# The buffers gh and gl are laid behind wsp, at the lower end of SBUF

## The chip, the cores and the metric

One core of a Trainium2 chip runs the kernel. The metric is device microseconds from start to end of one execution; the time shown is the median of three runs.

## What is computed

Three layers in a row, all in float32, from the reference (cut):

```
# q, k, v: (2, 8, 768, 64); block 32, window 16, nb = 24
k_sum = k.reshape(B, H, nb, block, D).max(axis=3)
v_sum = v.reshape(B, H, nb, block, D).mean(axis=3)
scores_l = scale * q @ k^T, kept where |i - j| < 16
scores_s = scale * q @ k_sum^T + log(block)
a = softmax of both side by side;  attn = a @ concat(v, v_sum)
x = attn.transpose(0, 2, 1, 3).reshape(1536, 512)
x = ((x @ w_a) * (x @ w_b)) @ w_out          # 512 -> 1536 -> 512
h = x @ w_in;  out = (h - tanh(h)) @ w_out2  # 512 -> 2048 -> 512
```

So it is a banded attention with block summaries, then a gated MLP, then a second MLP. The weights come to the kernel as words of 64 bits, which it decodes to float32 itself.

## The kernel before

**Precision by splitting.** A large matmul takes fp32r operands. Each operand is kept as two tiles, a rounded high part and the rest as a low part, and a product is three matmuls: high x high, high x low, low x high (lines 366 to 370, 397 to 398, 458 to 459). The tile `wsp` (four buffers of 4 KB per partition) holds the two parts of one weight tile, made by `split_w` (lines 181 to 186: ACT writes the high part, DVE or POOL the low one). XA and XB (16 KB each) hold the two parts of the activations of one block. `gh` and `gl` (two buffers of 2 KB each) hold the high and low parts of the hidden activations between the two products of an MLP; line 363 (ACT) writes `gh` and line 364 (DVE) writes `gl`.

**Positions.** The 1536 rows are three blocks of 512. The list `pos` (lines 478 to 507) is the order of work on TensorE. One position is twelve matmuls of 128x128 by 512 on one weight tile:

- `pos_a` and `pos_b` (lines 373 and 381): x times a tile of w_a or w_b into the PSUM banks pa and pb, through `proj` on line 370. Weights are wsp, the moving operand is XA (blocks 0 and 2) or XB (block 1). `pos_b` then multiplies both and splits the result into gh and gl.
- `pos_o` (line 390): the second product of the first MLP, line 398. Weights are wsp, the moving operand is gh or gl. There are 12 such positions in each block, 36 in all.
- `pos_h` (line 419): the first product of the second MLP, again line 370, into pa, pb, ps and pt in turn. Activations are in XB (blocks 0 and 2) or XA (block 1). The activation function h - tanh(h) is worked out on ACT and DVE, and the result g is split by `late_hi_lo` (line 444) one position later.
- `pos_o2` (line 448): the second product of the second MLP, line 459. Here the activations are the weights of the matmul and wsp is the moving operand. There are 48, one for each group G, two groups behind `pos_h`.

Where g of the second MLP is kept goes by the group's number:

```
439  gs[1000 + G] = pair((("gh", 2), ("gl", 2)) if G % 3 < 2 else (("vw", 3), ("vw", 3)))
```

`vw` is a buffer of the attention stage (three of 2 KB) that is free by then. So of every three groups two use gh and gl, and the third uses two of the vw buffers.

**Stages.** The first 45 us or so are the head: loads, and the first eight attention units, whose order on every engine is written out by hand (SEQ, line 771). In the head, gh and gl also serve as `at` tiles of four units, and ta and tg as `e` tiles (lines 667 and 700). Then positions run; until about 290 us the remaining 16 attention units are put in between, by the table `at` that `plan` fills (lines 520 to 575), and weights are loaded on SP's queue, decoded on ACT, DVE and POOL (lines 146 to 168) and, in part, written back and loaded again later. From position 0 on SP keeps the order as written while the framework's scheduler orders the other engines; from position 72 on all engines keep the order as written (line 498).

**Where buffers lie.** All tiles come from one pool. A tag gets its buffers, side by side, at the moment it is first used in the program, and each tag follows the one before it. By the program's allocation, in KB of the 224 KB of a partition, before the change:

```
qbd   24.3   wsp  28.3 to 44.3    XB  44.3 to 60.3    kw  60.3
w     64.3   vw  136.3 to 142.3   XA 142.3 to 158.3   kt 158.3
x20a 170.7   stage 178.7          x21a 190.7          e  198.7
ta   202.9   tg  206.9 to 210.9   gh 210.9 to 214.9   gl 214.9 to 218.9
at   218.9 to 222.9
```

Within 256 bytes, wsp, XB, vw and XA start at byte 32; gh and gl (and all tags from x20a on, as kt is 12,672 bytes) start at byte 160.

Of the kernel before, what the change touches and what calls it, by code (L numbers as in the profile page):

```python
# [12 lines left out]
F32R = mybir.dt.float32r  # L13
# [26 lines left out]
def band_attention_moe_kernel(ctx: ExitStack, tc: tile.TileContext, q, k, v, w_a, w_b, w_out, w_in, w_out2, out):  # L40
# [11 lines left out]
    TB = 512  # L52
# [10 lines left out]
    def st(shape, tag, bufs=1, dt=F32):  # L63
        return sb.tile(shape, dt, tag=tag, bufs=bufs, name=tag)
# [10 lines left out]
    mavp = st([128, KW + 2 * NB - 8], "qn", 3)  # L75
    qbd = st([128, 2, NP, 128], "qbd")
    qbd2 = st([128, 2, NP, 128], "wsp", 4)

    xb = st([128, 2 * KC * TB], "XB")
    kq = xb[:, 0:3072].rearrange("p (c h d) -> p c h d", c=NC, h=H)  # L80
# [753 lines left out]
```

## Time and profile before

| what | value |
| --- | --- |
| median of three runs | 667.28 us (665.36 to 667.33) |
| span of the profiled execution | 664.0 us |
| PE busy (matmuls) | 643.2 us, 97% |
| PE weight loads busy | 518.1 us, 78% |
| DVE busy | 501.9 us, 76% |
| ACT busy | 476.2 us, 72% |
| POOL busy | 209.7 us, 32% |
| granted TensorE clock, mean | 0.997 |

The profile is of one execution; its span is the time from the first to the last instruction, and the runs' times contain a little more around it. Busy shares are averages over stages. A matmul's duration in the profile reaches from its start to its modelled end and overlaps the next one, so twelve matmuls of some 390 ns each take 2.7 us together; the pace is read from the starts, or from the chain in order of time, where a row "PE acc L459 x12" is one position.

### The profile page before, as it was taken

What the parts mean: (1) busy time and instruction counts of PE and PEld (TensorE: products, weight loads), DVE (VectorE), ACT (ScalarE), POOL (GpSimd) and SP (SyncE); (2) the same over time, 40 slices, a digit from 0 to 9 for tenths busy, and PEclk for the clock granted to TensorE, in tenths of its full rate; (3) what the DMA queues carried; (4) which work ended last, traced back from release to release, by engine and by line L of the source; (5) the groups of instructions that cost most, each with busy time, mean ns of one, the idle gap of its engine ahead of it and who ended that gap; (6) DMA issues with size and microseconds to landing.
All of it is one profiled execution on the core that took longest, in us unless ns stands there. A gap on an engine that the chain in (4) does not pass through costs nothing.

```text
span 664.0 us, 9626 instructions
## 1 busy us (share of the span) xinstructions
PE 643.2 (97%) x3240; PEld 518.1 (78%) x3240; DVE 501.9 (76%) x999; ACT 476.2 (72%) x1000; POOL 209.7 (32%) x221
## 2 busy tenths in 40 slices
PE   7778999999899999999999999999999999999997
PEld 5567876888588888888888888888888888888885
DVE  5899999888675777647877748877777877777775
ACT  4899897798677687636655547777777777777774
POOL 6761231122000010101111135554444544444441
PEclk9989999999999999999999999999999999999999
DMA  9996984563414545513444200000010000000001
GB/s 203 243 237 179 250 226 128 169 216 107 102 66 124 169 152 155 144 47 112 149 140 152 68 1 0 1 0 1 1 63 1 0 1 0 32 33 1 1 0 64
DMA packets 84781, 62.11 MB, mean 94 GB/s; under 512 B 51892, under 2 KB 75444, under 8 KB 84732
## 3 DMA queue, kind: packets, MB, share of 16 engines
q1 hardware_dynamic: 84732, 61.50, 33.4%
q8 instruction: 25, 0.41, 0.3%
q14 instruction: 24, 0.20, 0.1%
HBM read 54.00 MB, written 7.34 MB: 92 GB/s over the span
## 4 chain that ended last, share of the span: by engine, by line
PE 82%; DVE 7%; ACT 4%; DMA 3%; issue 2%; SPq 1%; POOL 0%; DVEq 0%; ACTq 0%
PE acc L459 20%; PE pb L370 18%; PE pa L370 17%; PE acc L398 12%; PE pt L370 5%; PE ps L370 5%; DMA stage<-in_moe_w_in_dram 2%; PE ps L288 1%; DVE w L164 1%; PE ps L340 1%; DVE w L165 1%; PE pt L240 1%; PE pt L327 1%; DMA x20a<-in_q_dram 1%; SPq L610 1%
## 5 line engine op out<-in xcount | busy, mean ns | idle before, releaser
L185 POOL TENSOR_TENSOR wsp<-w,wsp 128x512 fp32r<-128x512 f32 x97 | 127.5, 1333 | 143.7 <-ACT wsp L184 143.7
L184 ACT ACTIVATE wsp<-w 128x512 fp32r<-128x512 f32 x201 | 121.4, 622 | 18.8 <-PE acc L398 8.6
L185 DVE TENSOR_TENSOR wsp<-w,wsp 128x512 fp32r<-128x512 f32 x104 | 75.0, 723 | 42.5 <-ACT wsp L184 42.3
L179 POOL TENSOR_SCALAR w<-w 128x512 f32<-128x512 f32 x52 | 42.0, 811 | 184.3 <-ACT w L154 184.1
L398 PE MATMUL acc<-gh,wsp 128*128 128x512 f32 x288 | 97.8, 398 | 0.5 <-ACT gh L363 0.5
L370 PE MATMUL pa<-XA,wsp 128*128 128x512 f32 x336 | 85.0, 400 | 2.8 <-ACT XA L720 2.1
L370 PE MATMUL pb<-XA,wsp 128*128 128x512 f32 x336 | 84.1, 394 | 1.4 <-DVE tg L386 1.4
L459 PE MATMUL acc<-wsp,gh 128*128 128x512 f32 x256 | 80.5, 396 | 0.0
L370 PEld LDWEIGHTS pa<-XA,wsp 128*128 128x128 f32 x336 | 63.5, 191 | 18.3 <-ACT XA L720 2.4
L370 PEld LDWEIGHTS pb<-XA,wsp 128*128 128x128 f32 x336 | 62.1, 188 | 15.0 <-ACT x21a L155 1.6
L363 ACT ACTIVATE gh<-tg 128x512 fp32r<-128x512 f32 x68 | 42.4, 623 | 33.3 <-DVE tg L386 32.9
L398 PEld LDWEIGHTS acc<-gh,wsp 128*128 128x128 f32 x288 | 53.7, 188 | 12.0 <-ACT gh L363 0.6
L370 PE MATMUL pb<-XB,wsp 128*128 128x512 f32 x240 | 61.0, 396 | 0.0
L370 PE MATMUL pa<-XB,wsp 128*128 128x512 f32 x240 | 60.4, 395 | 0.0
L398 PE MATMUL acc<-gl,wsp 128*128 128x512 f32 x144 | 57.3, 399 | 1.1 <-DVE gl L364 1.1
L459 PEld LDWEIGHTS acc<-wsp,gh 128*128 128x128 f32 x256 | 48.2, 188 | 11.1
L364 DVE TENSOR_TENSOR gl<-tg,gh 128x512 fp32r<-128x512 f32 x68 | 46.6, 686 | 9.4 <-ACT gh L363 9.3
L370 PEld LDWEIGHTS pa<-XB,wsp 128*128 128x128 f32 x240 | 44.5, 188 | 9.8 <-DVE XB L348 0.2
L370 PEld LDWEIGHTS pb<-XB,wsp 128*128 128x128 f32 x240 | 44.4, 188 | 9.5
L459 PE MATMUL acc<-wsp,gl 128*128 128x512 f32 x128 | 50.5, 394 | 0.0
L459 PE MATMUL acc<-wsp,vw 128*128 128x512 f32 x192 | 46.5, 390 | 0.0
L459 PEld LDWEIGHTS acc<-wsp,vw 128*128 128x128 f32 x192 | 35.9, 188 | 8.1 <-DVE vw L364 0.4
(304 smaller groups left out, 1176.0 us busy)
## 6 DMA issues: line engine op xcount, KB each, us to landing
stage<-in_moe_w_out_dram SPq DMA_DIRECT2D x19, 512.0 KB, 3.8
stage<-in_moe_w_in_dram SPq DMA_DIRECT2D x16, 512.0 KB, 5.6
stage<-in_moe_w_a_dram SPq DMA_DIRECT2D x8, 512.0 KB, 4.9
w<-wsc SPq DMA_DIRECT2D x16, 256.0 KB, 3.5
vw<-in_v_dram SPq DMA_DIRECT2D x19, 192.0 KB, 3.2
stage<-in_moe_w_b_dram SPq DMA_DIRECT2D x7, 512.0 KB, 5.7
wsc<-x21a SPq DMA_DIRECT2D x8, 256.0 KB, 4.9
wsc<-x21b SPq DMA_DIRECT2D x8, 256.0 KB, 5.1
```

The costliest lines, as they stand in the source:

```text
L164: nc.vector.scalar_tensor_tensor(r, t[:, :, 1], -0x40000000, r, op0=ALU.bitwise_and, op1=ALU.bitwise_or)
L165: nc.vector.tensor_tensor(r, r, t[:, :, 0], op=ALU.add)
L179: nc.gpsimd.tensor_scalar(rf, rf, HI_HI, HI_LO, op0=ALU.min, op1=ALU.max)
L184: nc.scalar.activation(s[:, 0, :], r, AF.Copy)
L185: eng.tensor_tensor(s[:, 1, :], r, s[:, 0, :].bitcast(F32), op=ALU.subtract)
L240: mm(pp, mavg[:, NB - 4 - 4 * c : 2 * NB - 4 - 4 * c], vch.pop(c).rearrange("p h d -> p (h d)"), start=(c == 0), stop=(c == NC - 1),)
L288: mm(pp[:, p, 0:NK], qt[:, p, :], kw[:, p, :], start=True, stop=True)
L363: nc.scalar.activation(dst[0], src, AF.Copy)
L364: eng.tensor_tensor(dst[1], src, dst[0].bitcast(F32), op=ALU.subtract)
L370: mm(dst, w, xx, start=(kk == 0 and n == 0), stop=(kk == KC - 1 and n == 2))
L398: mm(acc[blk][d][:, c0:c1], w, t, start=(f == 0 and c0 == 0 and n == 0), stop=(f == F1 - 1 and n == 2))
L459: mm(a[c], g[:, cs], s[:, i, :], start=(f == 0 and n == 0), stop=(f == F2 - 1 and n == 2))
```

## The change

Four tiles are reserved right after wsp is first used, two of gh and two of gl, and nothing is ever written to or read from these four. As the tags are then first used there, their buffers lie behind wsp (gh 44.3 to 48.3 KB, gl 48.3 to 52.3 KB), and every tag from XB to tg lies 8 KB higher: XB 52.3 to 68.3, vw 144.3 to 150.3, XA 150.3 to 166.3, ta and tg 210.9 to 218.9 KB. `at` stays where it was. No instruction is added, taken away or altered but for the addresses.

```
@@ -75,6 +75,9 @@
     mavp = st([128, KW + 2 * NB - 8], "qn", 3)
     qbd = st([128, 2, NP, 128], "qbd")
     qbd2 = st([128, 2, NP, 128], "wsp", 4)
+
+    for tag in ("gh", "gh", "gl", "gl"):
+        st([128, TB], tag, 2, F32R)
 
     xb = st([128, 2 * KC * TB], "XB")
     kq = xb[:, 0:3072].rearrange("p (c h d) -> p c h d", c=NC, h=H)
```

## Rows read from the trace of the kernel before

**Rows 1.** The page's first line: the profiled execution
```profile
span 664.0 us, 9626 instructions
```

**Rows 2.** Stretches: us, PE, PEld, DVE, ACT, POOL busy, clock, DMA share, GB/s
```profile
45.00:175.00 130.00, 126.30 (x684) 98.47 (x683) 119.00 (x267) 108.33 (x250) 30.30 (x35) 0.99 0.65 179
175.00:290.00 115.00, 113.48 (x665) 92.41 (x664) 75.39 (x192) 81.13 (x199) 10.38 (x15) 1.00 0.45 132
290.00:400.00 110.00, 110.00 (x481) 90.10 (x480) 78.03 (x121) 60.70 (x107) 18.48 (x22) 1.00 0.28 94
400.00:660.00 260.00, 260.00 (x1130) 211.90 (x1128) 194.87 (x297) 193.58 (x341) 120.52 (x92) 1.00 0.03 10
```

**Rows 3.** Groups by line, PE, 403:651 us (xcount, busy us, mean ns, idle)
```profile
L459 PE MATMUL acc<-wsp,gh 128*128 128x512 f32 x240 | 75.5, 396 | 0.0
L459 PE MATMUL acc<-wsp,gl 128*128 128x512 f32 x120 | 47.3, 394 | 0.0
L459 PE MATMUL acc<-wsp,vw 128*128 128x512 f32 x180 | 43.2, 389 | 0.0
L370 PE MATMUL pt<-XB,wsp 128*128 128x512 f32 x96 | 23.3, 391 | 0.0
```

**Rows 4.** Chain in order of time, 403:436 us (start us, us, what)
```profile
403.13 2.80 PE acc L459 x12
405.92 2.76 PE pt L370 x12
408.68 2.80 PE acc L459 x12
411.48 2.75 PE pa L370 x12
414.23 2.72 PE acc L459 x12
416.95 2.73 PE pb L370 x12
419.67 2.80 PE acc L459 x12
```

**Rows 5.** Timeline of PE, 403:422 us: two kinds of L459 position
```profile
408.52 0.64 PE L459 MATMUL acc<-wsp,gh 128*128 128x512 f32 x2
...
414.06 2.88 PE L459 MATMUL acc<-wsp,vw 128*128 128x512 f32 x12
```

**Rows 6.** Chain in order of time, 293:320 us
```profile
298.63 2.79 PE acc L398 x12
301.43 2.73 PE pa L370 x12
304.16 2.72 PE pb L370 x12
```

**Rows 7.** One position near the end, columns as in rows 2
```profile
654.20:656.70 2.50, 2.50 (x12) 1.88 (x10) 1.76 (x3) 0.74 (x2) 0.00 (x0) 1.00 0.00 0
```

**Rows 8.** Timeline of PE, 654:657 us, the same position
```profile
654.42 0.40 PE L459 MATMUL acc<-wsp,gl 128*128 128x512 f32 x1
...
656.52 0.40 PE L459 MATMUL acc<-wsp,gl 128*128 128x512 f32 x1
```

**Rows 9.** Line 398 alone: us, PE, PEld busy, clock, DMA share, GB/s
```profile
45.00:175.00 130.00, 38.68 (x144) 26.14 (x144) 0.99 0.65 179
175.00:290.00 115.00, 31.40 (x120) 22.11 (x120) 1.00 0.45 132
290.00:400.00 110.00, 41.36 (x168) 31.53 (x168) 1.00 0.28 94
```

**Rows 10.** Groups by line, whole run: line 459 on gh
```profile
L459 PE MATMUL acc<-wsp,gh 128*128 128x512 f32 x256 | 80.5, 396 | 0.0
```

**Rows 11.** Chain, shares by line, 45:175 us and then 175:290 us
```profile
by line: PE pb L370 13.2%; PE acc L398 10.9%; PE pa L370 10.6%; DMA stage<-in_moe_w_in_dram 8.1%; DVE w L164 6.8%; issue 6.3%; DVE w L165 4.6%; PE pt L240 4.0%; DVE wsp L185 3.9%; DMA stage<-in_moe_w_b_dram 3.2%; DVE w L161 2.5%; PE ps L288
...
by line: PE pa L370 29.4%; PE pb L370 29.0%; PE acc L398 24.5%; PE ps L288 6.2%; PE ps L340 4.9%; PE pt L327 3.0%; PE pt L269 1.8%; ACT wsp L184 0.5%; issue 0.5%; ACT at L330 0.4%
```

More of the change, by code (lines that the diff above doesn't have):

```diff
@@ L77, in band_attention_moe_kernel @@
     qbd2 = st([128, 2, NP, 128], "wsp", 4)
+    for tag in ("gh", "gh", "gl", "gl"):
+        st([128, TB], tag, 2, F32R)
     xb = st([128, 2 * KC * TB], "XB")
```

## The prediction

> **What bounds the kernel now.** I read the page's first line, then busy time by stretch, then the groups of one stretch on PE, and last the chain in order of time, where one position of the kernel (twelve matmuls on one weight tile) stands as one row. The profiled execution spans 664.0 us [rows 1]; the median of the three runs is 667.28 us, 3.3 us above that span, and I carry this difference along unchanged. The reader should see in the stretches that PE is busy for all of 290 to 660 us at full granted clock, while DVE, ACT and POOL stay at 75% or less [rows 2]. From 175 to 290 us it is busy for 98.7%, and the chain there is 98.8% PE [rows 2, 11]. Only from 45 to 175 us does the chain also run through weight loads and decoding; the PE entries with a share beside them add to 39% [rows 11]. So for most of the run the time is the number of matmuls times their pace, and a change that moves no instruction can matter only by changing that pace.
>
> The pace is not the same everywhere. In the second MLP a position of line 459 takes 2.80 us twice and 2.72 us the third time [rows 4]. The timeline tells which is which: the position from 408.5 us takes its weights from gh and gl, the one from 414.1 us from vw [rows 5]. Line 439 sends each third group through vw and the other two through gh and gl. The twelve matmuls are the same in count, size, moving operand (wsp) and PSUM banks (acc). By groups, a matmul lasts 396 ns on gh, 394 ns on gl and 389 ns on vw, over 540 of them and with no idle time ahead [rows 3]. The position of line 370 that follows gh takes 2.75 to 2.76 us, the one after vw 2.73 us [rows 4], so part of the cost is paid by the neighbour: its mean is 391 ns [rows 3]. In the first MLP gh and gl are the moving operand instead of the weights, and it is the same: 2.79 us on line 398 against 2.72 us for pb, and 2.73 us for the pa in between [rows 6]. What gh and gl have in common in both places is where they lie: 210.9 to 218.9 KB, near the top of the 224 KB of a partition, while wsp, XB, vw and XA, which run at 2.72 us per position, lie between 28.3 and 158.3 KB. (gh and gl also start 160 bytes behind a multiple of 256, those others 32 bytes behind one; the change alters both properties, so the forecast needs no choice between them.)
>
> That it is contention with the engines that fill these buffers is hard to hold: near the end, in a position on gh with POOL idle and ACT busy for 0.74 of 2.50 us [rows 7], nine matmuls still take 2.10 us [rows 8], which is 0.233 us each or 2.80 us for twelve, as in the busy middle.
>
> **The change, part by part.** It adds four tile reservations with no instruction behind them, so nothing is issued, no DMA joins SP's queue, and no wait is added that anything could queue behind: the two buffers of each tag are reserved twice, which leaves their alternation as it was. I price this at nothing; if it did alter a wait, the stretches in which PE never idles would show it at once.
>
> *gh and gl move from 210.9 to 44.3 KB.* They take the lower half of the place where XB lies today. With wsp weights, XB is the moving operand there and its matmuls cost 391 ns even with gh's tail in the mean [rows 3]; so this very place is known to be good for the moving operand. For the weights the nearest row is vw at 389 ns [rows 3]. I take 2.72 us for every position, the row that both uses share, and no better: no row shows a faster one.
>
> - Second MLP: three groups from 403.13 to 419.67 us take 16.54 us [rows 4]; six positions at 2.72 us are 16.32 us. The 48 groups hold sixteen such triples: 16 x 0.22 = 3.5 us. Gh alone has 256 matmuls on line 459 [rows 10], eight per position, so 32 positions, which agrees.
> - First MLP from 290 us: 2.79 + 2.73 + 2.72 = 8.24 us [rows 6] against 8.16 us, and 0.01 us from rounding as the next triple starts 8.25 us later; 0.09 us for each of 168/12 = 14 positions [rows 9]: 1.3 us.
> - 175 to 290 us: 120/12 = 10 positions [rows 9], 0.09 us each, nearly all on the chain [rows 11]: 0.9 us.
> - 45 to 175 us: 144/12 = 12 positions [rows 9], 1.1 us at most. Where PE saves time here, it often just waits for weights still being loaded and decoded, so I take the 39% that the chain shows of PE [rows 11]: 0.4 us. Bounds are nothing and 1.1 us.
>
> Sum: 3.5 + 1.3 + 0.9 + 0.4 = 6.1 us. The span would be 657.9 us, and the median 667.3 - 6.1 = 661.2 us. The cover is thin elsewhere: with PE 1% faster, ACT and DVE (75% and below after 290 us [rows 2]) are still not next; what is late next is PE again.
>
> *Everything from XB up to tg moves up by 8 KB* (`at`, above gl, stays). XA goes from 142.3 to 150.3 KB, so its upper half, the low parts of x, enters 158.3 to 166.3 KB, where no matmul of this size reads today. vw ends at 150.3 KB, below XA's present end. If gh's cost comes from height, the bound lies somewhere between 158.3 and 210.9 KB, and the 8 KB that XA newly enters are 15% of that; if it comes from the 160 bytes, XA keeps its 32 and nothing happens. I price XA at nothing and keep the other end as a rival. ta and tg now reach into gh's old place, but the large matmuls never read them, and no row shows ACT or DVE caring about the place. In the first 45 us gh and gl also serve four attention units; at 0.08 us each this is 0.3 us at the very most, either way, and I put it at nothing.
>
> A rule speaks against all of this. The Trainium skill, page "SBUF — State Buffer", section "Who interferes with whom", says that PE never waits on anyone because its ports are its own, and the page gives no price for an address. By that the move would be worth nothing and the time 667.3 us. The row with POOL idle agrees that it is no contention, but the pair of gh and vw positions does not agree that place is free. Its chance is that of the first rival.
>
> **The rivals.**
>
> *The place is not the cause.* Something else that goes with gh and gl (which instructions fill them, which semaphores their matmuls see) makes 2.80 us, and it moves with them: 667.3 us. For it: no engine's own row prices an address. Against it: the two MLPs use gh in opposite roles, with different producers' timing, and pay nearly the same 0.07 to 0.08 us in the position itself [rows 4, 6]; vw is filled by the same two lines 363 and 364. Chance 0.09.
>
> *XA's upper half becomes what gh was.* The first MLP has 48 pa and pb positions on XA (blocks 0 and 2, twelve each twice) and the second MLP 16 (block 1): 64. Four of twelve matmuls read the low part, so the price is 64 x 4/12 x 0.08 = 1.7 us if only they pay, and 64 x 0.09 = 5.8 us if each upset costs a whole position: 662.9 to 667.0 us. For it: the following positions do pay for an upset [rows 4]. Against it: only 15% of the possible bounds. Chance 0.08, most of it still faster by over 2 us.
>
> *The two reads of one matmul collide, and it is slower.* gh and gl then lie wall to wall with wsp, and each of the 36 + 32 = 68 positions reads one from each. If PE's weight read and its moving read hinder each other when both come from one part of memory, these positions keep a cost. It decides at 2.83 us: from there 68 x 0.03 = 2 us are lost beyond today's 2.80. If the present excess of 0.08 us doubled, it would be 68 x 0.08 = 5.4 us and 672.7 us. Against it: XB with wsp is just such a pair of neighbours today and costs 391 ns like the others [rows 3]. Chance 0.04.
>
> *The reservation does not do what it says,* and gh and gl stay on top or the order of instructions changes a little: about 667.3 us. Chance 0.02.
>
> **How the numbers follow.** The forecast has 0.77. A measurement of this kernel can tell about 0.3%, 2 us, from no change. Faster by more than that (below 665.3 us): the forecast and 0.06 of XA's case, 0.83. Within: 0.09 + 0.02 and 0.02 of XA's case, 0.13. Slower: the collision, 0.04. The lower end takes the 45 to 175 us stretch in full (660.5 us) and the spread of the runs, whose lowest is 1.9 us under the median: 658.8 us. The upper end takes in about half of XA's case: 665.0 us. Left out are the two cases without effect, the collision and the rest of XA, 0.19 in all.
>
> **What would show it.** Right: every line 459 position at 2.72 us, whether on gh or vw; line 398 at 2.72 us; gh, gl and vw groups within 1 ns of each other; PE's instruction count and the order of work unchanged; the stretch from 290 us shorter by 4.8 us. XA's case would show as 2.75 us or more for pa and pb on XA but 2.72 us on XB. The collision would show as line 398 and 459 above 2.80 us. The forecast is wrong if gh's positions still stand at 2.80 us, or if PE, now faster, shows new idle time ahead of line 370 or 459 behind ACT's wsp (line 184).

## The result and the profile after

The changed kernel takes 660.88 us (median of six runs, 659.02 to 661.90), the kernel before 666.79 us in the six runs made by then: 5.9 us less, ratio 0.9916 (95% interval 0.9898 to 0.9934). The forecast was 661.2 us, faster. The profiled execution spans 657.7 us against 664.0 us [rows 1], 6.3 us less. Every engine runs the same instructions in the same order as before; line numbers are higher by 3.

The page's first line, and its busy times by engine:

```profile
span 657.7 us, 9626 instructions
...
PE 637.2 (97%) x3240; PEld 518.0 (79%) x3240; DVE 502.4 (76%) x999; ACT 475.3 (72%) x1000; POOL 209.3 (32%) x221
```

PE's busy time falls from 643.2 to 637.2 us with the same 3240 matmuls; no other engine's changes by over 1 us. So the matmuls themselves became cheaper. Groups by line on PE, 400 to 648 us, as in [rows 3]:

```profile
L462 PE MATMUL acc<-wsp,gh 128*128 128x512 f32 x250 | 77.0, 389 | 0.0
L462 PE MATMUL acc<-wsp,gl 128*128 128x512 f32 x125 | 48.7, 389 | 0.0
L462 PE MATMUL acc<-wsp,vw 128*128 128x512 f32 x180 | 43.2, 389 | 0.0
L373 PE MATMUL pt<-XB,wsp 128*128 128x512 f32 x96 | 23.1, 389 | 0.0
```

gh (396 ns before), gl (394) and the neighbours on XB (391) are all at the 389 ns that vw alone had. The chain in order of time, around 300 us and from 400 us, as in [rows 6] and [rows 4]:

```profile
296.82 2.72 PE acc L401 x12
299.54 2.72 PE pa L373 x12
302.26 2.72 PE pb L373 x12
...
400.18 2.72 PE acc L462 x12
402.90 2.72 PE pt L373 x12
405.62 2.72 PE acc L462 x12
408.34 2.72 PE pa L373 x12
411.06 2.72 PE acc L462 x12
413.78 2.72 PE pb L373 x12
```

Every position from 290 us up to the last two is at 2.72 us; the two in three at 2.80 us and their followers at 2.75 to 2.76 us are gone.

Where the time was won is read by laying the same piece of work side by side. First the chain before, at the transposes of line 269 that end the wait near 175 us, then the chain after:

```profile
177.27 0.58 PE pt L269 x4
```
```profile
176.24 0.59 PE pt L272 x4
```

That is 1.0 us by then, in this pair of executions. The L398 position that starts at 298.63 us [rows 6] starts at 296.82 us: 1.8 us. The first one of line 459, at 403.13 us [rows 4], starts at 400.18 us: 2.95 us. And the last, on the timeline of PE before and then after:

```profile
656.78 3.29 PE L459 MATMUL acc<-wsp,vw 128*128 128x512 f32 x12
```
```profile
650.44 3.33 PE L462 MATMUL acc<-wsp,vw 128*128 128x512 f32 x12
```

6.3 us, and that stays to the end. By stretch the gain is 1.0, 0.8, 1.1 and 3.4 us.

### The profile page after: what moved, and what is told of

Read it like the earlier page. It is cut to its first block, busy times and chain, and to the rows that moved or that the text cites. A ratio compares the mean times of both kernels' runs of the same rounds, so it can differ in the third digit from the quotient of the medians.

```text
span 657.7 us, 9626 instructions
## 1 busy us (share of the span) xinstructions
PE 637.2 (97%) x3240; PEld 518.0 (79%) x3240; DVE 502.4 (76%) x999; ACT 475.3 (72%) x1000; POOL 209.3 (32%) x221
## 4 chain that ended last, share of the span: by engine, by line
PE 87%; DVE 6%; ACT 3%; DMA 2%; issue 1%; SPq 1%; POOL 0%; DVEq 0%
PE acc L462 20%; PE pb L373 19%; PE pa L373 18%; PE acc L401 14%; PE pt L373 5%; PE ps L373 5%; PE ps L291 2%; PE ps L343 1%; DMA stage<-in_moe_w_in_dram 1%; PE pt L330 1%; PE pt L243 1%; DMA x20a<-in_q_dram 1%; SPq L613 1%; DVE w L167 1%; DVE w L168 1%
## 5 line engine op out<-in xcount | busy, mean ns | idle before, releaser
L462 PE MATMUL acc<-wsp,gh 128*128 128x512 f32 x256 | 78.8, 389 | 0.0
```

Source lines behind the costliest of these rows:

```text
L462: mm(a[c], g[:, cs], s[:, i, :], start=(f == 0 and n == 0), stop=(f == F2 - 1 and n == 2))
```

## The experiments

The forecast left open what about the place counts. The theory **height** says that gh and gl were slow because they lay near the top. The rival **offset** says that it was because they started 160 bytes behind a multiple of 256, where wsp, XB, vw and XA start at 32. The change altered both. In all kernels below no instruction is added, taken away or reordered; only addresses differ, through reservations that nothing uses. All ratios are to the kernel before, run on the same chip.

**Same height, other offset** (the kernel before, with):

```
         elif n.startswith("T3e"):
             i = int(n[3])
+            if i == 2:
+                st([128, 32], "pad")
```

> The kernel before with 128 unused bytes ahead of gh: gh and gl stay near the top (211.0 to 219.0 KB) but start 32 bytes behind a multiple of 256 instead of 160; nothing else moves but at. Theory height: positions of lines 398 and 459 on gh and gl stay at 2.80 us, ratio to before 1.00. Rival offset (the 160 bytes are the cause): they fall to 2.72 us, ratio 0.991, some 661 us.

Measured: 660.61 us, ratio 0.9917 (0.9897 to 0.9938). Its chain, around 300 us and from 400 us:

```profile
298.42 2.72 PE acc L398 x12
301.14 2.72 PE pa L370 x12
...
401.78 2.72 PE acc L459 x12
404.50 2.72 PE pt L370 x12
```

128 unused bytes do all that the change does, with gh and gl still at the top. Height falls.

**Low, but at 160** (the changed kernel, with one line ahead of the new loop and one behind it):

```
+    st([128, 32], "pad0")
     for tag in ("gh", "gh", "gl", "gl"):
         st([128, TB], tag, 2, F32R)
+    st([128, 32], "pad1")
```

> The changed kernel with 128 unused bytes ahead of gh and 128 behind gl: gh and gl lie low (44.4 to 52.4 KB) but start 160 bytes behind a multiple of 256; XB, vw and XA keep their 32. Theory height: all positions 2.72 us as after the change, ratio to before 0.991. Rival offset: positions on gh and gl are 2.80 us again, ratio to before 1.00.

Measured: 665.83 us, ratio 1.0009 (0.9996 to 1.0021). Its chain shows the positions of before, digit for digit, at the low place:

```profile
299.04 2.79 PE acc L403 x12
301.83 2.73 PE pa L375 x12
...
403.53 2.80 PE acc L464 x12
406.33 2.76 PE pt L375 x12
```

**Everything from wsp up moved by 128 bytes** (the kernel before, with one line ahead of wsp; wsp, XB, vw and XA then start at 160, gh and gl at 32):

```
+    st([128, 32], "pad")
     qbd2 = st([128, 2, NP, 128], "wsp", 4)
```

> The kernel before with 128 unused bytes ahead of wsp: everything from wsp up moves by 128 bytes, so wsp, XB, vw and XA start at 160 and gh and gl, still near the top, at 32. Theory height: as before, 2.80 us on gh and gl, 2.72 us elsewhere, ratio 1.00. Rival offset taken by itself: gh no longer costs as such, but every position reads wsp at 160, so all 201 positions go to about 2.80 us, some 10 us slower, ratio 1.015. Rival offset of the two operands against each other: unchanged, ratio 1.00, as the difference stays 128.

Measured: 665.33 us, ratio 0.9999 (0.9985 to 1.0012). In its chain gh, now at 32, still costs 2.80 us, and vw against wsp, both now at 160, costs 2.72 us:

```profile
404.20 2.80 PE acc L460 x12
...
415.30 2.72 PE acc L460 x12
```

So neither operand's own start counts, but the difference between the two.

**How large a difference.** gh and gl get buffers of 2304 bytes in the changed kernel and are used from byte s on; here s = 32 (8 elements):

```
     for tag in ("gh", "gh", "gl", "gl"):
-        st([128, TB], tag, 2, F32R)
+        st([128, TB + 64], tag, 2, F32R)
...
-        return [st([128, TB], t, n, F32R) for t, n in tags]
+        return [st([128, TB + 64], t, n, F32R)[:, 8 : 8 + TB] if t[0] == "g" else st([128, TB], t, n, F32R) for t, n in tags]
```

> The changed kernel, gh and gl in buffers of 2304 bytes and used from byte 32 on, so that they start 32 bytes further behind a multiple of 256 than wsp. Theory bit (only whether both operands start in the same half of 256 bytes counts): both start in the lower half, 2.72 us, ratio to before 0.991. Theory distance (the cost grows with the difference up to 128): part of the cost, positions between 2.72 and 2.80 us. Theory any (every difference costs): 2.80 us, ratio 1.00.

> The same with gh and gl used from byte 64 on, 64 bytes off wsp. Theory bit: 2.72 us, ratio 0.991. Theory distance: about half of the cost, 2.76 us, ratio 0.995. Theory any: 2.80 us, ratio 1.00.

> The same with gh and gl used from byte 192 on, 192 bytes off wsp. Theory bit: the other half of 256 bytes, 2.80 us, ratio 1.00. Theory distance (192 is 64 the other way round): as the 64-byte run, 2.76 us. Theory any: 2.80 us, ratio 1.00.

> The same with gh and gl used from byte 256 on. If the cost goes by 256 bytes, there is none: 2.72 us, ratio 0.991. If it goes by 512 or more, 2.80 us, ratio 1.00. It is also the control of the longer buffers, which move XB and what follows by another 1 KB.

> The changed kernel, gh and gl in buffers of 2304 bytes and used from byte 16 on. Theory any, down to single bytes: 2.80 us as with 32 bytes, ratio to before 1.00. Theory grain (only steps of 32 bytes count): 2.72 us, ratio 0.991.

Measured ratios: s = 16: 0.9937 (0.9918 to 0.9957); 32: 1.0007 (0.9995 to 1.0020); 64: 0.9995 (0.9979 to 1.0011); 192: 0.9967 (0.9953 to 0.9981); 256: 0.9911 (0.9885 to 0.9937). Positions from the chains, line 401 (gh moving) first, line 462 (gh as weights) second; s = 16, 32, 64, 192 and 256 in this order:

```profile
290.28 2.78 PE acc L401 x12
...
403.02 2.72 PE acc L462 x12
```
```profile
291.88 2.80 PE acc L401 x12
...
405.09 2.79 PE acc L462 x12
```
```profile
289.70 2.76 PE acc L401 x12
...
402.53 2.80 PE acc L462 x12
```
```profile
298.28 2.80 PE acc L401 x12
...
402.94 2.75 PE acc L462 x12
```
```profile
296.26 2.72 PE acc L401 x12
...
399.62 2.72 PE acc L462 x12
```

None of the four theories on record holds whole. "Bit" fails at 32 and 64, "distance" at 32 (which costs as much as 128), "any" at 16, 64 and 192, where one of the two lines is cheaper or free, and "grain" at 16, where line 401 pays. What fits is a difference with a sign: call d the moving operand's start minus the weights' start, modulo 256. Line 401 has d = s, line 462 has d = 256 - s. Then the rows order themselves: d = 0: 2.72 us; 16: 2.78; 32: 2.80; 64: 2.76 (as moving, s = 64) and 2.75 (as weights, s = 192); 128: 2.79 and 2.80 (the kernel before); 192: 2.80 in both roles; 224: 2.79; 240: 2.72. At 64, 128 and 192 the two roles agree to 0.01 us, so there it is the difference and not the role that sets the cost. At 16, 32, 224 and 240 only one role was seen, so that 240 is free as such, and not only with gh as weights, is not shown. This ordering was found after the runs and not forecast.

**Another buffer out of step** (the changed kernel, with one line ahead of XA; kt and what follows move along, gh and gl don't):

```
+        st([128, 32], "pad0")
         XAv = st([128, 4, 2 * TB], "XA")
```

> The changed kernel with 128 unused bytes ahead of XA: XA, whose positions are at 2.72 us in both kernels, starts at 160, and gh, gl, vw, XB and wsp at 32. Theory difference of the two operands of a matmul, whichever buffer: the 64 positions on XA go to 2.80 us with what follows them, XB, gh and vw keep 2.72 us unless they come right behind one; 64 x 0.08 = 5.1 us slower than after the change, ratio to before some 0.998. Rival (only gh and gl are sensitive): ratio 0.991.

Measured: 664.56 us, ratio 0.9975 (0.9960 to 0.9990). In the chain the positions on XA now cost what those on gh did, while XB's at 400 us are untouched:

```profile
292.51 2.79 PE pa L373 x12
295.30 2.80 PE pb L373 x12
...
400.59 2.72 PE ps L373 x12
403.31 2.72 PE acc L462 x12
...
476.75 2.79 PE pa L373 x12
479.54 2.73 PE acc L462 x12
```

So the sensitivity is not gh's and gl's own. By the two ratios to the kernel before, 0.9975 and 0.9916, it costs some 3.9 us, less than the 5.1 us expected. That sum counts in full the 24 positions on XA that run before 175 us, where PE also waits for weights; from 176 us on, where the other 40 positions on XA lie, matmul by matmul the run falls 3.4 us behind the changed kernel, and 40 x 0.08 is 3.2 us.

**Every position out of step** (the changed kernel, with wsp alone at 160):

```
+    st([128, 32], "pad0")
     qbd2 = st([128, 2, NP, 128], "wsp", 4)
 
+    st([128, 32], "pad1")
     for tag in ("gh", "gh", "gl", "gl"):
```

> The changed kernel with 128 unused bytes ahead of wsp and 128 behind it: wsp alone starts at 160, gh, gl, XB, vw and XA at 32, so that every one of the 201 positions reads two operands that differ by 128. Theory difference: every position costs 2.79 to 2.80 us, also on vw and XB, 201 x 0.075 = 15 us over the changed kernel, some 676 us, ratio to before 1.014. Rival (wsp's start does not count, only that of the activations): as after the change, ratio 0.991.

Measured: 672.85 us, ratio 1.0109 (1.0089 to 1.0129), some 13 us over the changed kernel by the two ratios. The pace is as expected to 0.01 us, on gh, vw and XB alike; by the timeline the row from 417.85 us is on vw:

```profile
406.68 2.79 PE acc L464 x12
409.47 2.79 PE pt L375 x12
412.26 2.80 PE acc L464 x12
...
417.85 2.80 PE acc L464 x12
420.65 2.80 PE pb L375 x12
```

The sum was put too high (15 us). From 290 us on, matmul by matmul, the run falls 9.7 us behind the changed kernel, and the 133 positions there at 0.075 us make 10.0 us; ahead of 290 us it falls 3.7 us behind, where the other 71 positions, counted in full, would make 5.3 us. Part of PE's time there is a wait for something else [rows 11]. (The matmuls make 204 positions, 2448 / 12, and not 201.)

**Does the common start count?** (the changed kernel, with 224 unused bytes ahead of wsp: `st([128, 56], "pad")`)

> The changed kernel with 224 unused bytes ahead of wsp: wsp, gh, gl, XB, vw and XA all start on a multiple of 256. Theory difference: nothing changes, 2.72 us, ratio to before 0.991. Rival (the distance from a multiple of 256 counts too): the common pace itself moves off 2.72 us; 1 ns for each of 2448 matmuls would be 2.4 us.

Measured: 660.12 us, ratio 0.9902 (0.9870 to 0.9933). In its chain a position on gh is at 2.72 us (the line above wsp makes line 462 into 463):

```profile
401.58 2.72 PE acc L463 x12
```

The common start does not count.

**The other large buffers that PE reads, aligned too** (the changed kernel, with 160 unused bytes ahead of ident, 96 behind it and 128 behind kt):

> The changed kernel with unused bytes ahead of and behind ident and behind kt, so that every large buffer that PE reads (ident, e, at, x20 too) starts 32 bytes behind a multiple of 256. Theory any, carried to the attention units: the slow matmuls that follow an attention unit in the first 290 us go too, some 1.4 us in all (the matmul starts of the changed kernel that are 228 to 245 ns apart add to 1.43 us over the common pace), 659.5 us, ratio 0.989. Rival (those come from the units' own shapes, and their pace isn't changed): as after the change, ratio 0.991.

Measured: 659.50 us, ratio 0.9907 (0.9876 to 0.9939), which can't be told from the change's. The starts of its matmuls say more: those 228 to 245 ns apart add to 1.40 us over the common pace, against 1.43 us. So the slow matmuls behind an attention unit do not go by where these buffers start. That no difference of starts is at work in them is not shown: lines 291 and 330 of the changed kernel read kw and e in steps of 480 bytes (120 words of 4), so of four such operands three stay out of step wherever the buffer starts. No version tried beats the changed kernel beyond its interval.

## Why the prediction was right

**The mechanism as far as it was forecast holds.** PE's pace is the time, gh and gl slowed it, and the change brings them to the pace of vw: 2.72 us in each position, to the digit. New idle time of PE, named as a sign against it, shows once and is small: ahead of the last position, which waits for ACT's vw (line 366), two starts are 406 ns apart against 264 before, 0.14 us.

**The terms of the sum**, by the pieces laid side by side: second MLP 3.5 us forecast, 3.4 measured; first MLP 1.2 us for the 13 positions from 298.63 us on, against 1.1; and 1.0 us for the eleven positions from 175 us to there, against 0.8. By the starts of the same matmuls in the other kernels that keep every position in step (gh and gl at the top but at 32, s = 256, the common start moved, the other buffers aligned), these three pieces give 3.4, 1.15 and 0.6 to 0.8 us. So the forecast was some 0.4 us too high there, out of 5.7.

What lies ahead was forecast at 0.4 us and gave 1.0 us in this pair. One pair of executions does not size it. The same transposes with gh and gl at the top and in step, and then low and out of step:

```profile
177.87 0.59 PE pt L269 x4
```
```profile
177.68 0.59 PE pt L274 x4
```

The first of these kernels has the pace of the changed one and still arrives later than the second, and 0.6 us later than the kernel before; with s = 256 they come 1.6 us earlier. Whether the 39% of PE in the chain was a fair measure of this stretch stays open. The sum was 6.1 us, the span gave 6.3, the medians 5.9: that it fits so closely is in part luck. (The lower end of the range was also added up wrongly: 660.5 less 1.9 is 658.6 us, not 658.8.)

**The moves priced at nothing** were worth nothing: XA and XB in their new places run at 2.72 us, and DVE's and ACT's busy times hardly move.

**The rivals.** "The place is not the cause" falls as it was priced, as the move did bring the time; but what counts about the place is only where a buffer starts against its partner. XA's case rested on height, and its upper half, now at 158.3 to 166.3 KB, costs nothing; that buffer can be slowed, yet by 128 bytes and not by 8 KB. The collision of neighbours did not show: gh and wsp lie wall to wall at 2.72 us. Yet this rival, with a chance of 0.04, had the kind of cause nearest to what was found, two reads of PE that hinder each other; what it had wrong is that lying in one part of memory brings it about. The forecast named height first and the 160 bytes in a parenthesis, and needed no choice between them; had it been asked to choose by the order in which it told them, it would have chosen wrong.

**The rule that spoke against it.** By the Trainium skill, page "SBUF — State Buffer", section "Who interferes with whom", PE waits on no one; that agrees so far as no other engine is needed for the cost, but the page has no price for addresses, and here there is one of 0.08 us on 2.72. The Trainium skill's page "TensorE: Matmul & The Clock Gate", section "Step-by-step: what each phase is for", says that loading the next weights takes no read bandwidth from the running matmul. If that were all, the two starts could not matter to each other; the runs show that they do, and at a difference of 128 the rows that follow place the start of the cost at that very load.

**Own weights or the next one's?** Within a position all weights start alike, but where one position follows another the kernel before tells them apart. Its last matmul of pb ahead of a position on gh in the second MLP, the weights load beside it, and gh's first matmul:

```profile
419.28 0.40 PE L370 MATMUL pb<-XB,wsp 128*128 128x512 f32 x1
419.28 0.19 PEld L459 LDWEIGHTS acc<-wsp,gh 128*128 128x128 f32 x1
419.51 0.40 PE L459 MATMUL acc<-wsp,gh 128*128 128x512 f32 x1
```

Both operands of that pb matmul start at 32, the weights loaded beside it at 160. From its start to the next one it takes 232 to 233 ns at each of the 31 such places from 290 us on, against 226.7 ns at the common pace; this is the 0.01 us by which pb at 416.95 us [rows 4] exceeds 2.72, although it follows vw and not gh. Where gh is the moving operand, the last matmul ahead of it keeps 226 to 227 ns, and the slow spacing begins with gh's own first matmul, at 234 or 235 ns. Both fit if the moving reads of one matmul meet the load of the next one's weights; a meeting with its own weights fits only the second. That holds for 128. At s = 32 the matmul ahead of gh as weights is slow too, 235 ns, but at s = 64 and 192 it takes 225 to 226 ns and the slow spacing begins one matmul later, so for those differences this stays open. The end of a position tells less: in the kernel before, the slow spacing runs on for three to seven matmuls.

**What stays open:** why a difference of starts costs, and why 16 and 240 cost differently. Only nine values of d were tried (one of them, 256, that counts as 0), and no matmul of another type or width.

## What to carry to other kernels

In a stream of fp32r matmuls with new weights each time, let the tiles that serve as weights and as moving operands start at the same byte modulo 256; a table of the program's addresses shows it at once, and some unused bytes put it right. Look for it when the same matmul has two paces by buffer alone in the profile, and compare like positions in the chain. An odd-sized buffer (here kt, 12,672 bytes = 49.5 x 256) puts everything behind it out of step.

## What was not expected of the hardware

The pace of TensorE depends on the difference between its two operands' start addresses: 2.72 us for twelve matmuls of 512 columns at a difference of 0, 2.75 to 2.80 us at 16, 32, 64, 128, 192 and 224, and 2.72 us again at 240 (seen only with gh as the weights), at a granted clock of 1.00 from 175 us on [rows 2]. At a difference of 128 the cost begins where the moving reads of one matmul run beside the load of the next one's weights: 232 to 233 ns to the next start against 226.7. And a position in step that follows one out of step still pays 0.01 to 0.04 us [rows 4, 6] before it is back at the common pace.
